# The last gate tile moves from GpSimd to VectorE, and eleven of 37 groups of heads change places

## Chip, cores and metric

The kernel runs on one core of one Trainium2 chip. The metric is the device time of one execution in microseconds (us), lower is better. The engines are called PE (TensorE), ACT (ScalarE), DVE (VectorE), POOL (GpSimd) and SP (SyncE, here only a DMA queue).

## What is computed

```python
xn = layernorm(x)                       # x: 1 x 2048 x 448, bf16
qkv = xn @ wqkv                         # 16 heads of 28
p = softmax(q @ k^T * 28**-0.5)         # 16 x 2048 x 2048
s = (p @ v) @ wo
g = silu(gelu(xn @ w1 + b1) @ w2 + b2)  # 448 -> 1792 -> 448
out = x + s * g
```

## The kernel before

**Blocks and groups.** The 16 heads are cut in four groups of four heads (g), the 2048 queries in four chunks of 512 (c). A block is one g with one c, so there are 16 blocks, run in the order b = 4g + c. A block holds 64 score tiles m of 128 keys by 512 queries: 16 key tiles times four heads. Four consecutive m, one for each head, are a group of heads q = m // 4; block b holds the groups 16b to 16b + 15. The last block is cut into narrower query pieces so that its parts finish one after the other.

**Two ways to take an exponential.** Most score tiles go from PE through PSUM to ACT: the process `p_exps` reads alternately three and two PSUM banks (512 columns each) with one ACTIVATE (line 1303). The 37 groups listed in `QUADS` (line 31) are left out of that stream (`step`) and are "late" groups: `p_late` starts one when the score stream has reached it (`K.next_m >= m0`, somewhat earlier during the GELU phase) and three work units of memory are free. DVE then computes the exponential: four TENSOR_SCALAR of 128x512 (line 1406, `p_apass`), and four instructions over 128x2048 (lines 1466, 1468, 1469, 1470, `p_expq`). A late group yields three tiles instead of one for the second matmul, so its product with v costs PE three times as many matmuls (`pv_task`, line 1542). A block's sum in the PSUM tile `acc` is complete only when all of its late groups have been added; then DVE copies it out (line 1595, `p_epi`; line 1569, `p_epi4`, for the three parts of the last block), and the next block may use `acc`.

**Order.** The order in which each engine gets its instructions is not written by hand. A planner at build time keeps a model of each engine's time, a duration and a rank for each task, and always puts next the task that can start first (`run`, `start_of`, `put`). Each engine then executes its list in that order and waits on semaphores. A change to one task, or to `QUADS`, can so reorder everything that is planned behind it. The process `p_busy` gives PE small dummy matmuls (line 919, three at a time, added to `acc` with zeros) where the model shows PE too idle; they stop when the scores are nearly at their end.

**The phases.** After loading and normalisation, blocks 0 to 8 run beside the first dense matmul (line 1111). In block 9, ACT leaves the exponentials for the GELU (line 1160). Blocks 9 to 12 run beside the second dense matmul (line 1181), whose rows end in the gate g: tanh on ACT (line 1197), then one DVE instruction. The last blocks run beside the output matmul (line 1634).

**The tail.** For the last chunk of rows (c = 3) the gate of the tiles t = 0, 1, 2 is made early. The tile t = 3 waits until the last exponential has been planned, because tanh would stand in ACT's way: tanh on ACT (line 1213), product on POOL (1215), sum on POOL (1217). In `p_epi4` and `p_norm4` the last part of the last block goes: copy out of `acc` (DVE, 1569), broadcast of the sums (PE, 1580), RECIPROCAL (DVE, 1583), product (DVE, 1586). Then `p_last` and `t_oev`: the last output matmul (PE, 1634), product with the gate (DVE, 1643), plus x (DVE, 1647), and the store (SP, 1649). The product at 1643 for t = 3 needs the gate tile t = 3 (`K.b_g3`).

`K.E_done` counts the blocks whose copy out of `acc` has been planned; it reaches `NBLK + 1` with the copy of the last part. `K.on4[3]` becomes true when the product at 1586 for t = 3 has been planned.

Of the kernel before, what the change touches and what calls it, by code (L numbers as in the profile page):

```python
# [8 lines left out]
ALU = mybir.AluOpType  # L9
ET = mybir.EngineType  # L10

PE, ACT, DVE, POOL, SP = ET.PE, ET.Activation, ET.DVE, ET.Pool, ET.SP
# [14 lines left out]
NBLK = G * C  # L27
MTOT = NBLK * T * 4

GM = 64 * 9 + 6  # L30
QUADS = (17, 21, 24, 33, 39, 49, 52, 66, 75, 85, 86, 98, 100, 114, 124, 134, 138, 142, 146, 153, 154, 155, 161, 162, 171, 178, 179, 189, 194, 197, 206, 210, 211, 225, 227, 237, 243)
SM_SCALE = DH ** -0.5
LOG2E = 1.4426950408889634
EXP_C, EXP_LC = 0.1669921875, 1.1155446
# [44 lines left out]
class _Kernel:  # L79
# [314 lines left out]
    def schedule(self):  # L394
# [28 lines left out]
        K.pv_done = [False] * MTOT  # L423
        K.late = {4 * q + k for q in QUADS for k in range(4)}
        K.late_left = [sum(1 for q in QUADS if K.sub_of(4 * q) == b) for b in range(NBLK + 3)]
        K.late_on = False
# [765 lines left out]
    def p_silu(self, c):  # L1192
        K = self
        yield ("until", lambda: K.f2n[c] == 4 and K.ready([K.b_fsb[c % 2]], 0.3) and (c < 2 or K.g_done[c - 2]))
        fb, sg = K.fsb[:, c % 2, :, :], K.sig[:, c % 2, :, :]
        nt = 4 if c < C - 1 else 3
        yield _Task(ACT, lambda eng: eng.activation(sg[:, 0:nt, :], fb[:, 0:nt, :], ACTF.Tanh, scale=0.5),
                    [K.b_fsb[c % 2]], [K.b_sig[c % 2]], 0.1 + 0.375 * nt, 0.0, 0)
        for t0 in range(0, nt, 2):
            t1 = min(t0 + 2, nt)  # L1200
            yield _Task(DVE, lambda eng, t0=t0, t1=t1: eng.scalar_tensor_tensor(
                K.g_sb[:, c, t0:t1, :], sg[:, t0:t1, :], 1.0, fb[:, t0:t1, :], op0=ALU.add, op1=ALU.mult),
                        [K.b_sig[c % 2], K.b_fsb[c % 2]], [K.b_h[c], K.b_g[c]], 0.15 + 0.467 * (t1 - t0), 0.0, 3)
        K.g_done[c] = True
        if c < C - 1:
            return
        K.b_x2[c].r = list(K.b_h[c].r) + [K.b_h[c].w]
        K.dma(SP, lambda eng: eng.dma_start(K.x2[:, c, :, :], K.A_x[0].rearrange("(c p t) d -> c p t d", p=128, t=4)[c]),
              K.s_x2[c], writes=[K.b_x2[c]])
        if nt < 4:  # L1210
            yield ("until", lambda: K.exp_m == MTOT - 1)
            o = K.g_sb[:, c, 3, :]
            yield _Task(ACT, lambda eng: eng.activation(sg[:, 3, :], fb[:, 3, :], ACTF.Tanh, scale=0.5),
                        [K.b_fsb[c % 2]], [K.b_sig3], 0.47, 0.0, 0)
            yield _Task(POOL, lambda eng: eng.tensor_tensor(o, sg[:, 3, :], fb[:, 3, :], ALU.mult),
                        [K.b_sig3, K.b_fsb[c % 2]], [K.b_h[c], K.b_g3], 0.85, 0.05, 0)
            yield _Task(POOL, lambda eng: eng.tensor_tensor(o, o, fb[:, 3, :], ALU.add),
                        [K.b_fsb[c % 2]], [K.b_h[c], K.b_g3], 0.85, 0.05, 0)

    def pieces(self, m):  # L1220
        b, r = m // 64, m % 64
# [154 lines left out]
    def p_late(self):  # L1376
        K = self
        yield ("until", lambda: K.late_on)
        K.spawn(K.p_room(), 0)
        for q in QUADS:  # L1380
            m0 = 4 * q
# [346 lines left out]
```

## Time and profile before

| what | us |
|---|---|
| median of 7 runs | 458.36 (458.24 to 459.08) |
| the profiled execution, its time | 458.41 |
| its span from first to last instruction | 456.5 |
| granted PE clock, mean | 0.997 of full |
| PE busy | 431.2 (94%) |
| ACT busy | 441.0 (97%) |
| DVE busy | 369.8 (81%) |
| POOL busy | 69.9 (15%) |

The table is read so: the span lies in the profiled execution's own time, with 1.9 us around it. Busy times are sums over the whole span, and say only which engines are nearly full. Where an engine idles, and for whom, is in the timeline (start, duration, engine, line, what is written from what, count, and in brackets the idle time before it with what ended it), in the waits (who waited for whom), and in the busy times of stretches of the span.

### The profile page before, as it was taken

The page shows a single profiled execution, that of the slowest core. Times are in us where ns is not written, and L with a number is a line of the kernel's source. Part 1 is how long each engine was busy: PE and PEld are TensorE (multiplying, and loading weights), DVE is VectorE, ACT ScalarE, POOL GpSimd, SP SyncE. Part 2 cuts the span into 40 slices and gives each one's busy share as a digit, 9 for nine tenths or more (in the row PEclk, how much of TensorE's full clock was granted, in tenths as well). Part 3 has the DMA queues.
Part 4 walks back from the last instruction along what each step waited for, and adds up shares of the span by engine and source line. Part 5 has one row for each costly group of instructions (what it writes and reads, how often), then busy time and mean ns, then how long its engine had stood idle before and what let it go on. Part 6 is the DMA issues. An engine that isn't in the chain of part 4 may idle for free.

```text
span 456.5 us, 10602 instructions
## 1 busy us (share of the span) xinstructions
PE 431.2 (94%) x4397; PEld 159.9 (35%) x4428; DVE 369.8 (81%) x574; ACT 441.0 (97%) x403; POOL 69.9 (15%) x123
## 2 busy tenths in 40 slices
PE   6999999999999999999999999999999999999995
PEld 4543323333233332323234333343333333334552
DVE  8956898958978787967879887378899889988866
ACT  6999999999999999999999998999999999999993
POOL 7470100110020101000010112020011010212211
PEclk9999999999999999999999999999999999999998
DMA  8701000000000000000040000000000000313012
GB/s 272 258 3 37 1 0 1 1 12 2 3 1 0 1 1 3 2 1 1 1 142 3 1 1 1 1 2 0 1 1 2 1 1 0 64 20 41 4 23 62
DMA packets 8049, 11.16 MB, mean 24 GB/s; under 512 B 1697, under 2 KB 6993, under 8 KB 7954
## 3 DMA queue, kind: packets, MB, share of 16 engines
q1 hardware_dynamic: 6850, 8.43, 5.8%
q0 software_dynamic: 864, 1.38, 2.5%
q8 instruction: 35, 0.57, 0.6%
q10 hardware_dynamic: 288, 0.69, 0.4%
q14 instruction: 12, 0.10, 0.1%
HBM read 8.61 MB, written 3.21 MB: 26 GB/s over the span
## 4 chain that ended last, share of the span: by engine, by line
PE 61%; ACT 24%; issue 9%; DVE 4%; DMA 1%; SPq 0%; POOL 0%; ACTq 0%; DVEq 0%; POOLq 0%
PE ring L1247 18%; ACT P L1303 13%; PE acc L1542 12%; ACT h L1303 8%; PE misc L1181 7%; PE ring L1111 6%; PE acc L919 4%; PE ring L1181 3%; PE ring L758 2%; PE misc L1111 2%; PE misc L758 1%; ACT xnT L1303 1%; PE misc L1634 1%; PE ring L1634 1%; DMA h<-in_A_wqkv_dram 1%
## 5 line engine op out<-in xcount | busy, mean ns | idle before, releaser
L1303 ACT ACTIVATE P<-ring 128x1024 bf16<-128x1024 f32 (+1 forms) x187 | 216.5, 1276 | 1.2 <-PE ring L1247 1.0
L1247 PE MATMUL ring<-qT,kT 32*128 32x512 bf16 (+2 forms) x1078 | 145.1, 358 | 10.0 <-ACT P L1303 4.5
L1303 ACT ACTIVATE h<-ring 128x1024 bf16<-128x1024 f32 (+1 forms) x102 | 118.5, 1270 | 0.4 <-PE ring L1247 0.2
L1247 PEld LDWEIGHTS ring<-qT,kT 32*128 32x128 bf16 x1078 | 37.3, 91 | 131.7 <-ACT P L1303 55.9
L1303 ACT ACTIVATE xnT<-ring 128x1536 bf16<-128x1536 f32 (+1 forms) x68 | 78.9, 1294 | 0.4 <-PE ring L1247 0.4
L1542 PE MATMUL acc<-P,vaug 128*32 128x512 bf16 (+2 forms) x530 | 49.1, 355 | 0.0
L1111 PE MATMUL ring<-xnT,w 128*128 128x512 bf16 x164 | 44.5, 381 | 2.7 <-issue 1.4
L1478 POOL TENSOR_SCALAR cv<-vaug 128x128 bf16<-128x128 bf16 x38 | 24.6, 647 | 138.3 <-PE acc L1542 136.4
L1607 POOL CAST rhi<-rc 128x16 bf16<-128x16 f32 x15 | 8.1, 537 | 200.8 <-DVE rc L1605 144.5
L1181 PE MATMUL misc<-w,h 128*128 128x448 bf16 x154 | 37.6, 356 | 0.0
L919 PE MATMUL acc<-ident,zero 128*128 128x128 bf16 x366 | 31.0, 220 | 0.0
L1542 PE MATMUL acc<-h,vaug 128*32 128x512 bf16 x248 | 28.3, 384 | 0.0
L1247 PE MATMUL misc<-qT,kT 32*128 32x512 bf16 (+1 forms) x74 | 27.7, 377 | 0.0
L919 PEld LDWEIGHTS acc<-ident,zero 128*128 128x128 bf16 x366 | 21.1, 98 | 14.6 <-issue 12.9
L1406 DVE TENSOR_SCALAR kT<-ring 128x512 uint16<-128x512 f32 x27 | 18.6, 688 | 4.6 <-PE ring L1247 4.5
L1111 PEld LDWEIGHTS ring<-xnT,w 128*128 128x128 bf16 x180 | 13.4, 97 | 21.9 <-issue 8.0
L1406 DVE TENSOR_SCALAR x_sb<-misc 128x512 uint16<-128x512 f32 x22 | 15.1, 687 | 5.6 <-PE misc L1247 5.5
L1406 DVE TENSOR_SCALAR w<-misc 128x512 uint16<-128x512 f32 x18 | 12.4, 688 | 8.4 <-PE misc L1247 8.3
L1094 DVE CAST h<-ring 128x512 bf16<-128x512 f32 x23 | 15.7, 684 | 2.8 <-PE ring L1111 2.6
L1542 PEld LDWEIGHTS acc<-P,vaug 128*32 128x32 bf16 x530 | 12.1, 95 | 15.9 <-issue 13.2
L1181 PEld LDWEIGHTS misc<-w,h 128*128 128x128 bf16 x154 | 11.2, 97 | 18.4 <-issue 11.1
L1542 PE MATMUL acc<-xnT,vaug 128*32 128x512 bf16 (+2 forms) x222 | 17.1, 332 | 0.2 <-DVE E_sb L1595 0.2
(288 smaller groups left out, 678.7 us busy)
## 6 DMA issues: line engine op xcount, KB each, us to landing
w<-in_B_w_dram SPq DMA_DIRECT2D x1, 1568.0 KB, 7.4
w<-in_B_w_dram SPq DMA_DIRECT2D x1, 1344.0 KB, 8.4
out_dram<-in_A_x_dram SPq DMA_DIRECT2D x3, 448.0 KB, 10.8
out_dram<-h POOLq DMA_DIRECT2D x6, 224.0 KB, 3.9
x_sb<-in_A_x_dram SPq DMA_DIRECT2D x2, 448.0 KB, 4.7
h<-in_A_wqkv_dram SPq DMA_DIRECT2D x3, 168.0 KB, 5.1
x_sb<-in_A_x_dram ACTq DMA_DIRECT2D x1, 448.0 KB, 5.3
h<-in_A_x_dram SPq DMA_DIRECT2D x1, 448.0 KB, 3.3
```

The source lines that it names most:

```text
L758: ins = eng.matmul(bank, w[:, kt, g * 128:(g + 1) * 128], K.xnT[:, kt, c * 512:(c + 1) * 512], start=(kt == 0), stop=(kt == KT - 1))
L919: ins = eng.matmul(K.acc[:, 0:128], K.zero[:, :], K.ident[:, :], start=False, stop=True, skip_group_check=True)
L1094: yield _Task(DVE, lambda eng: eng.tensor_copy(dst, bank), [tok], wr, 0.69, 0.0, 2)
L1111: ins = eng.matmul(bank, K.w1[:, kt, ft * 128:(ft + 1) * 128], K.xnT[:, kt, c * 512:(c + 1) * 512], start=(kt == 0), stop=(kt == KT - 1))
L1181: ins = eng.matmul(ps, hv[:, ft, t * 128:(t + 1) * 128], K.w2[:, ft, :], start=(ft == 0), stop=(ft == FT - 1))
L1247: return eng.matmul(dst, K.kT[32 * j:32 * j + 32, g, t * 128:(t + 1) * 128], K.qT[32 * j:32 * j + 32, g, c * 512 + q0:c * 512 + q0 + nq], ...
L1303: return eng.activation(reg[:, i0:i0 + n, :], K.ring[:, b0:b0 + n, :], ACTF.Exp, scale=SM_SCALE)
L1406: yield _Task(DVE, lambda eng: eng.tensor_scalar(K.unit[u][:, 512 * k:512 * k + 512].bitcast(dt.uint16), bank, SM_SCALE * LOG2E * 128.0, ( ...
L1478: yield _Task(POOL, lambda eng, i=i, t=t: eng.tensor_scalar(K.cv[:, i, :], K.vaug[:, t, 4 * g:4 * g + 4, :].rearrange("p h e -> p (h e)"), ...
L1542: return eng.matmul(K.acc[32 * j:32 * j + 32, q0:q0 + nq], w, ap[:, col:col + nq], tile_position=(0, 32 * j), start=(t == 0), stop=(t == T ...
L1607: yield _Task(POOL, lambda eng: eng.tensor_copy(K.rhi[:, :], K.rc[:, :]), [K.b_rc], [K.b_rhl], 1.1, 0.0, 1)
L1634: ins = eng.matmul(ps, K.qT[:, g, c * 512 + t * 128:c * 512 + (t + 1) * 128], K.wo[:, g, :], start=(g == 0), stop=(g == G - 1))
```

## The change

The diff does two things. The two instructions that build the last gate tile go from POOL to DVE. Each gets a place of its own: the product is offered to the planner once the last copy out of `acc` has been planned, the sum once the product at 1586 for t = 3 has been planned. Their rank becomes 2. The tanh on ACT stays.

The list of late groups changes in twelve places of 37; eleven groups leave it and eleven enter (100 is in both). Each block keeps as many late groups as it had. In blocks 1, 5 and 6 groups move later (21 to 22; 85, 86 to 87, 88; 98, 100 to 100, 101), in block 8 one earlier (134 to 133), in block 9 155 becomes 157. In block 12 the groups 197, 206 become 201, 205, in block 13 211 becomes 216, in block 14 227, 237 become 231, 238.

```diff
-QUADS = (17, 21, 24, 33, 39, 49, 52, 66, 75, 85, 86, 98, 100, 114, 124, 134, 138, 142, 146, 153, 154, 155, 161, 162, 171, 178, 179, 189, 194, 197, 206, 210, 211, 225, 227, 237, 243)
+QUADS = (17, 22, 24, 33, 39, 49, 52, 66, 75, 87, 88, 100, 101, 114, 124, 133, 138, 142, 146, 153, 154, 157, 161, 162, 171, 178, 179, 189, 194, 201, 205, 210, 216, 225, 231, 238, 243)
...
             yield _Task(ACT, lambda eng: eng.activation(sg[:, 3, :], fb[:, 3, :], ACTF.Tanh, scale=0.5),
                         [K.b_fsb[c % 2]], [K.b_sig3], 0.47, 0.0, 0)
-            yield _Task(POOL, lambda eng: eng.tensor_tensor(o, sg[:, 3, :], fb[:, 3, :], ALU.mult),
-                        [K.b_sig3, K.b_fsb[c % 2]], [K.b_h[c], K.b_g3], 0.85, 0.05, 0)
-            yield _Task(POOL, lambda eng: eng.tensor_tensor(o, o, fb[:, 3, :], ALU.add),
-                        [K.b_fsb[c % 2]], [K.b_h[c], K.b_g3], 0.85, 0.05, 0)
+            yield ("until", lambda: K.E_done == NBLK + 1)
+            yield _Task(DVE, lambda eng: eng.tensor_tensor(o, sg[:, 3, :], fb[:, 3, :], ALU.mult),
+                        [K.b_sig3, K.b_fsb[c % 2]], [K.b_h[c], K.b_g3], 0.39, 0.0, 2)
+            yield ("until", lambda: K.on4[3])
+            yield _Task(DVE, lambda eng: eng.tensor_tensor(o, o, fb[:, 3, :], ALU.add),
+                        [K.b_fsb[c % 2]], [K.b_h[c], K.b_g3], 0.39, 0.0, 2)
```

## The prediction

> **What bounds the kernel now.** I read the page's busy times first, then the busy times by stretch, then who waited for whom on ACT, then the timeline of the tail and of two stalls.
>
> ```profile
> PE 431.2 (94%) x4397; PEld 159.9 (35%) x4428; DVE 369.8 (81%) x574; ACT 441.0 (97%) x403; POOL 69.9 (15%) x123
> ```
>
> ```profile
> 300.00:340.00 40.00, 39.32 (x354) 13.67 (x354) 34.25 (x48) 39.86 (x36) 5.80 (x9) 1.00 0.01 1
> 340.00:380.00 40.00, 39.56 (x388) 12.77 (x386) 35.31 (x48) 39.57 (x35) 4.25 (x7) 1.00 0.01 1
> 380.00:420.00 40.00, 37.66 (x440) 14.43 (x437) 37.02 (x53) 40.00 (x36) 7.12 (x11) 1.00 0.19 30
> ```
>
> The columns are the stretch, its length, and busy PE, weight loads, DVE, ACT, POOL, then the granted clock. ACT is the bound: it works from 12.6 us to 449.2 us almost without a pause. The change keeps 37 late groups, and as many in each block, so ACT keeps its 876 exponential tiles and its work; what the list can win is only ACT's idle time, what it can lose is open. In 340 to 380 ACT idles 0.43 us and PE is 99% busy: there the exponentials wait for scores that stand behind other matmuls.
>
> How much is there? The trace's starts and durations give the distance between the ends of consecutive ACT instructions: 1.34 us for three banks, 0.915 for two when nothing waits. The excess over this is 4.7 us over the whole run. 1.73 us of it fall on exponentials behind the first late group of the second third (152 us on), in eight places of over 0.08 us: 0.30 at 211.6, 0.22 at 223.2, 0.12 at 277.4, 0.24 at 333.7, 0.12 at 349.7, 0.35 at 362.9, 0.09 at 365.3, 0.29 at 376.9. Beside them GELU waits 2.0 us in two places (line 1160, for PE's line 1111), at its end near 272 and 275 us.
>
> **Part 1, the tail.** The timeline of the end:
>
> ```profile
> 449.04 0.39 DVE L1647 TENSOR_TENSOR h<-h 128x448 bf16<-128x448 bf16 x1
> 449.35 0.62 DVE L1643 TENSOR_TENSOR h<-misc,h 128x448 bf16<-128x448 f32 x1
> ...
> 449.73 1.03 POOL L1215 TENSOR_TENSOR h<-w 128x448 bf16<-128x448 bf16 x1 [5.18 <-ACT w L1213]
> ...
> 450.00 1.00 DVE L1647 TENSOR_TENSOR h<-h 128x448 bf16<-128x448 bf16 x1
> ...
> 450.16 0.34 PE L919 MATMUL acc<-ident,zero 128*128 128x128 bf16 x3
> 450.84 1.06 POOL L1217 TENSOR_TENSOR h<-h,w 128x448 bf16<-128x448 bf16 x1
> 450.93 0.28 DVE L1569 CAST E_sb<-acc 128x128 bf16<-128x128 f32 x1
> ...
> 451.53 0.96 DVE L1583 RECIPROCAL w<-ring 128x128 f32<-128x128 f32 x1 [0.32 <-PE ring L1580]
> 452.59 0.29 DVE L1586 TENSOR_TENSOR qT<-E_sb,w 128x128 bf16<-128x128 bf16 x1
> ...
> 453.34 0.62 DVE L1643 TENSOR_TENSOR h<-ring,h 128x448 bf16<-128x448 f32 x1 [0.46 <-PE ring L1634]
> ```
>
> The reader is to see one instruction at two prices: line 1647 takes 0.39 us at 449.04 and 1.00 at 450.00, where POOL's product runs beside it. The copy of the last block's sum (1569) stands behind it, and the rest of the chain (1580, 1583, 1586, 1634, 1643, 1647, store) behind that copy.
>
> Removed: two POOL instructions, 1.03 + 1.06 us. They need no cover, since POOL has nothing after them. What the first does to DVE goes: 1.00 - 0.39 = 0.61 us. But the copy also waits for `acc`, whose last writers are the dummies at 450.16, ending at 450.50; an earlier copy (440.55) started 0.06 behind the last matmul (440.10 + 0.39). So PE is late next: copy at 450.56 in place of 450.93, **0.37 us earlier**. The copy itself took 0.28 here and 0.23 at 444.17; I count nothing for that.
>
> The Trainium skill (GPSIMD Engine Reference, Specifications) says that POOL shares its SBUF interfaces with VectorE and contends with DVE instructions that have two SBUF inputs. The trace agrees, 0.39 against 1.00, and 1643, whose one input is PSUM, keeps 0.62 beside the same POOL instruction. By this rule alone one would count 0.61; the wait for PE makes it 0.37. Were the dummies planned elsewhere, up to 0.6.
>
> Added: two DVE products or sums of 128x448 bf16, nearest row 1647 alone, 0.39 each. The first stands between the copy and the reciprocal. In the new times the copy ends at 450.84, the reciprocal's input comes 0.32 later, at 451.16. Unrelated DVE instructions start some 0.07 before the one ahead ends (449.04 + 0.39 = 449.43, next start 449.35), so the product runs 450.77 to 451.16 and holds the reciprocal not at all. The skill speaks against this (VectorE: DVE Perf Modes, The DRAIN you can't avoid): the next operation does not start until the pipeline is empty. By that the product would end at 450.84 + 0.39 = 451.23 and cost 0.07; this trace's overlapping starts make it 0. I take the row. The second follows 1586 (452.59 + 0.29 = 452.88, less the 0.37) and its gap to 1643 is 0.46: 0.39 fits, cost 0. If the planner put the product behind the reciprocal instead, 1586 would be 0.32 later and the gain nearly gone. ACT's tanh ends at 449.64, ahead of either place. No DMA moves; the store at 1649 only comes earlier. The part is worth -0.37, bounds -0.6 and 0.
>
> **Part 2, the list.** An exact cost cannot be read off, because the planner reorders everything behind 21. It is bounded below by the idle time (1.73 plus at most 2.0 in the GELU) and from above only by new stalls. The early moves (21, 85, 86, 98, 100) lie where ACT hardly waits: I cost them at nothing, covered by ACT's queue of finished scores; without that cover, one stall like those listed, 0.1 to 0.35. The move 155 to 157 falls in the GELU phase, where groups up to 48 tiles ahead are admitted, so 157 (tile 628, 40 beyond 588) starts as 155 did: nothing. What remains is block 12:
>
> ```profile
> 376.90 2.36 ACT L1303 ACTIVATE xnT<-ring 128x1536 bf16<-128x1536 f32 x2 [0.18 <-PE ring L1247]
> ```
>
> ```profile
> 375.01 0.40 PE L1542 MATMUL acc<-kT,vaug 128*32 128x512 bf16 x4
> 375.24 0.39 PE L1542 MATMUL acc<-wk,vaug 128*32 128x512 bf16 x4
> 375.46 0.39 PE L1542 MATMUL acc<-x_sb,cv 128*32 128x512 bf16 x4
> 375.78 0.55 PE L1181 MATMUL misc<-w,h 128*128 128x448 bf16 x2
> 376.26 0.90 PE L1247 MATMUL ring<-qT,kT 32*128 32x512 bf16 x6
> ```
>
> Before the stall at 376.9 PE works off a late group's three products (12 matmuls) and a piece of the second dense matmul. Then come the scores: of the six in the last line, three start together at 376.26 and 376.27, a fourth starts at 376.49 and ends at 376.86, two more belong to the next exponential. The fourth is the last tile of late group 206, planned into the same task; its strip of the array was taken, so it runs 0.22 behind, and ACT, which waits for the whole task, starts at 376.90. At 362.29 it is the same with a tile of 197 (fourth matmul at 362.52, ACT at 362.93); the stall at 365.3 comes with 197's last tile. Both groups leave the list. So 0.35 + 0.09 + 0.29 = **0.73 us** are at places whose cause moves away; 201 and 205 may make stalls of their own. I take the 0.73 as won and no new stall, for behind 380 us, where PE has dummies to drop, ACT shows no excess with the six groups from 210 on.
>
> **Sum.** 458.41 - 0.37 - 0.73 = 457.31, so 457.3. The profiled execution stands 0.05 above the median, which changes nothing.
>
> **Rivals.** (B) The stalls only change places: in 340 to 380 PE stays 99% busy, and 201 and 205 again have last tiles that find their strip taken. Then the tail alone counts: 458.41 - 0.37 = 458.0, no measurable difference. For it speaks that stalls appear at groups that stay, too (349.7, 333.7).
>
> (C) Slower: block 14 finishes late. Its last late group goes from 237 to 238, behind 231, which starts later than 227 did. Before, 237 was scored on DVE from 417.6 and its last step stood at 425.8, 8.2 us; the block's copy came at 429.36, while PE filled 420 to 430 with 60 dummies for want of other work. A group is 4 x 0.448 = 1.8 us of ACT; 238 then starts near 420.5 and ends near 428.7, 2.9 us later, and the copy near 432.3. All products of the last block wait for this copy. PE behind it has only some 27 dummies at 0.063 us to drop, 1.7 us, and is otherwise full to 450. Past a delay of 1.7 us the rest shows at the end: 2.9 - 1.7 = 1.2, less 0.37: 458.41 + 0.83 = 459.2; with 231 still on DVE when 238 starts, one to two us more. Against it: with 227 moved, 231 and 238 no longer share DVE with a neighbour as 225 and 227 did, and 238 may take less than 8.2.
>
> (D) PE finishes the GELU's direct tiles earlier or later, as the plan falls: up to 2.0 less or about 1 more.
>
> **Chances.** Forecast 0.42, B 0.25, C 0.28, D 0.05, half to each side. I count 0.2% (0.9 us) as what a measurement of this kernel can tell from no change: faster is below 457.4, slower above 459.3. Part of the forecast's case misses 457.4 by a small new stall, part of B passes it by a small luck. Faster 0.45, same 0.27, slower 0.28. The forecast alone ranges from 456.6 to 457.9. Down, the range takes in both bounds of part 1 and the other stalls, 458.4 - 0.6 - 1.3; up, case C with one us more, 460.2, less the tenth left out: 456.5 to 459.9.
>
> **What will show it.** Line 1647 for t = 2 at 0.39 and the copy 1569 about 0.06 behind PE's last write of `acc`; the product ahead of 1583 with the gap there unchanged; from the last exponential's end (449.2) to the span's end 6.9 in place of 7.3. For part 2: ACT's idle time in 340 to 380 at 0.1 or less in place of 0.43, and the last exponential ending near 448.5. Wrong would be a last exponential at or after 449.2, new stalls in blocks 5 to 8, or block 14's copy behind 431 with a longer tail.

## The result, and the profile after

The changed kernel takes 457.10 us (median of 12 executions, 457.01 to 457.67) against 458.42 before (30 executions): ratio 0.9970, 95% interval 0.9963 to 0.9978, 1.3 us faster. The forecast was 457.3. The sum is right; hardly one of its terms is. The executions of the first experiment below fall in two groups, four at 457.86 to 457.97 (granted clock 0.997 or 0.998) and nine at 458.26 to 458.65 (0.996), and those of before beside it likewise, 22 at 458.24 to 458.56 (0.997 to 0.999) and nine at 458.64 to 459.06 (0.995 to 0.997), so that its median compares unlike with unlike: group against group the difference is 0.4 to 0.5.

The profiled execution took 457.43 us, its span 455.6. From line 1217 on, line numbers are two higher than before. The busy times, and the stretch in which ACT idled 0.43 us before:

```profile
PE 429.5 (94%) x4389; PEld 160.6 (35%) x4419; DVE 369.1 (81%) x576; ACT 441.2 (97%) x403; POOL 69.7 (15%) x121
```

```profile
340.00:380.00 40.00, 39.45 (x387) 13.09 (x379) 35.93 (x48) 39.79 (x35) 5.05 (x7) 1.00 0.01 1
```

ACT's work is what it was, and it idles 0.21 us there in place of 0.43. The tail, from the timeline (start, duration, engine, line):

```profile
447.57 0.62 DVE L1645 TENSOR_TENSOR h<-ring,h 128x448 bf16<-128x448 f32 x1
448.22 0.39 DVE L1649 TENSOR_TENSOR h<-h 128x448 bf16<-128x448 bf16 x1
449.30 0.29 DVE L1571 CAST E_sb<-acc 128x128 bf16<-128x128 f32 x1 [0.69 <-PE acc L1544]
449.51 0.38 DVE L1216 TENSOR_TENSOR h<-w 128x448 bf16<-128x448 bf16 x1
449.92 0.96 DVE L1585 RECIPROCAL w<-misc 128x128 f32<-128x128 f32 x1
450.98 0.29 DVE L1588 TENSOR_TENSOR qT<-E_sb,w 128x128 bf16<-128x128 bf16 x1
451.19 0.38 DVE L1219 TENSOR_TENSOR h<-h,w 128x448 bf16<-128x448 bf16 x1
451.49 0.62 DVE L1645 TENSOR_TENSOR h<-ring,h 128x448 bf16<-128x448 f32 x1
452.14 0.39 DVE L1649 TENSOR_TENSOR h<-h 128x448 bf16<-128x448 bf16 x1
452.45 0.62 DVE L1645 TENSOR_TENSOR h<-ring,h 128x448 bf16<-128x448 f32 x1
453.10 0.39 DVE L1649 TENSOR_TENSOR h<-h 128x448 bf16<-128x448 bf16 x1
```

The product (1216) and the sum (1219) stand where they were expected, and cost the reciprocal nothing. But two pairs 1645, 1649 now stand behind them, where before there was one. The first belongs to tile t = 2, whose last output matmul PE now makes at 449.18, behind the last products with v; in the kernel before that pair stood ahead of the copy. Each pair takes 0.96 us from start to start. So the copy stands 1.06 us behind the last exponential's end in place of 1.74, 0.68 earlier, but from the copy to the last product it is 3.15 us in place of 2.41, 0.74 more, since t = 2's pair now stands there.

So that the parts can be told apart, I cut every trace at five points into four parts: the start of the first exponential, the start of the first GELU ACTIVATE, the end of the last one, the end of the last exponential, and the end of the last DVE instruction (2.13 or 2.14 us before the span's end in all but one run). The load of the GELU's table, 1.28 us on ACT ahead of the first ACTIVATE, counts to the first part; the expectations below that speak of 28.9 and 27.75 us count it to the GELU. Starts and ends are the trace's.

| kernel | median us | to GELU | GELU | to last exponential | tail |
|---|---|---|---|---|---|
| before | 458.42 | 235.89 | 27.58 | 173.09 | 5.21 |
| changed | 457.10 | 236.06 | 26.45 | 172.79 | 5.25 |

The differences are +0.17, -1.13, -0.30 and +0.04, together -1.22; the first exponential of this execution starts 0.30 later (12.93 against 12.63), which is why its span is only 0.9 shorter. The gain lies in the GELU stretch, for which the prediction counted nothing; the tail, for which it counted 0.37, won nothing.

### The profile page after: what moved, and what is told of

It reads as the page before. It is cut to its first block, busy times and chain, and to the rows that moved or that the text cites. A ratio compares the mean times of both kernels' runs of the same rounds, so it can differ in the third digit from the quotient of the medians.

```text
span 455.6 us, 10592 instructions
## 1 busy us (share of the span) xinstructions
PE 429.5 (94%) x4389; PEld 160.6 (35%) x4419; DVE 369.1 (81%) x576; ACT 441.2 (97%) x403; POOL 69.7 (15%) x121
## 4 chain that ended last, share of the span: by engine, by line
PE 61%; ACT 26%; issue 10%; DVE 2%; POOL 1%; ACTq 0%; DVEq 0%; POOLq 0%
PE ring L1249 17%; ACT P L1305 14%; PE acc L1544 11%; ACT h L1305 8%; PE ring L1111 7%; PE misc L1181 5%; PE ring L1181 3%; PE misc L1111 3%; ACT xnT L1305 3%; PE acc L919 2%; PE misc L758 2%; PE ring L758 2%; PE ring L1636 2%; PE misc L1636 1%; PE acc L901 1%
## 5 line engine op out<-in xcount | busy, mean ns | idle before, releaser
L1480 POOL TENSOR_SCALAR cv<-vaug 128x128 bf16<-128x128 bf16 x38 | 26.5, 698 | 134.3 <-PE acc L1544 132.6
L1111 PE MATMUL ring<-xnT,w 128*128 128x512 bf16 x139 | 35.8, 380 | 2.1 <-issue 1.4
L1181 PE MATMUL ring<-w,h 128*128 128x448 bf16 x112 | 26.9, 355 | 0.0
L1181 PE MATMUL misc<-w,h 128*128 128x448 bf16 x112 | 26.9, 355 | 0.0
L1249 PE MATMUL misc<-qT,kT 32*128 32x512 bf16 (+1 forms) x68 | 25.3, 377 | 0.0
L1111 PE MATMUL misc<-xnT,w 128*128 128x512 bf16 x68 | 19.1, 382 | 0.3 <-issue 0.2
L1111 PEld LDWEIGHTS ring<-xnT,w 128*128 128x128 bf16 x152 | 12.2, 97 | 17.7 <-issue 5.6
L1408 DVE TENSOR_SCALAR w<-ring 128x512 uint16<-128x512 f32 x17 | 11.7, 685 | 5.9 <-PE ring L1249 5.9
L1160 ACT ACTIVATE h<-h 128x2048 bf16<-128x2048 bf16 (+2 forms) x8 | 16.2, 2021 | 0.0
L1408 DVE TENSOR_SCALAR x_sb<-ring 128x512 uint16<-128x512 f32 x19 | 13.1, 687 | 3.8 <-PE ring L1249 3.8
```

What stands on the lines that cost most here:

```text
L1111: ins = eng.matmul(bank, K.w1[:, kt, ft * 128:(ft + 1) * 128], K.xnT[:, kt, c * 512:(c + 1) * 512], start=(kt == 0), stop=(kt == KT - 1))
L1160: yield _Task(ACT, lambda eng, dst=dst, src=src: eng.activation(dst, src, ACTF.Gelu_apprx_tanh), rd, wr, 0.4267 * n + (0.1 if pc else 0.06 ...
L1181: ins = eng.matmul(ps, hv[:, ft, t * 128:(t + 1) * 128], K.w2[:, ft, :], start=(ft == 0), stop=(ft == FT - 1))
L1249: return eng.matmul(dst, K.kT[32 * j:32 * j + 32, g, t * 128:(t + 1) * 128], K.qT[32 * j:32 * j + 32, g, c * 512 + q0:c * 512 + q0 + nq], ...
L1408: yield _Task(DVE, lambda eng: eng.tensor_scalar(K.unit[u][:, 512 * k:512 * k + 512].bitcast(dt.uint16), bank, SM_SCALE * LOG2E * 128.0, ( ...
L1480: yield _Task(POOL, lambda eng, i=i, t=t: eng.tensor_scalar(K.cv[:, i, :], K.vaug[:, t, 4 * g:4 * g + 4, :].rearrange("p h e -> p (h e)"), ...
```

## The experiments

The medians of before beside the runs were 458.37 (e1 to e4, e12), 458.41 (e5 to e8) and 458.34 (e9 to e11).

**The tail alone.** The changed kernel with the old list:

```diff
-QUADS = (17, 22, 24, 33, 39, 49, 52, 66, 75, 87, 88, 100, 101, 114, 124, 133, 138, 142, 146, 153, 154, 157, 161, 162, 171, 178, 179, 189, 194, 201, 205, 210, 216, 225, 231, 238, 243)
+QUADS = (17, 21, 24, 33, 39, 49, 52, 66, 75, 85, 86, 98, 100, 114, 124, 134, 138, 142, 146, 153, 154, 155, 161, 162, 171, 178, 179, 189, 194, 197, 206, 210, 211, 225, 227, 237, 243)
```

> The new tail with the old list; the instruction orders of all engines up to the last exponential are those of before. Theory P (the prediction's terms): the copy out of acc comes 0.37 us earlier, about 0.06 behind the dummies, the product is hidden ahead of the reciprocal, the sum in the gap ahead of the last product: 458.42 - 0.37 = 458.05. Theory N (the tail brings nothing, since in the changed kernel the end follows the last exponential by 7.36 us as by 7.34 before): 458.4, and an end 7.3 us behind the last exponential. Should the product hold the reciprocal up (pipeline emptied first), 458.1.

Measured: 458.31 us, ratio 0.9996 (0.9988 to 1.0004); the tail takes 4.83 us in place of 5.21. Its timeline:

```profile
449.92 0.39 DVE L1649 TENSOR_TENSOR h<-h 128x448 bf16<-128x448 bf16 x1
450.46 0.29 DVE L1571 CAST E_sb<-acc 128x128 bf16<-128x128 f32 x1
450.66 0.38 DVE L1216 TENSOR_TENSOR h<-w 128x448 bf16<-128x448 bf16 x1
451.07 0.96 DVE L1585 RECIPROCAL w<-ring 128x128 f32<-128x128 f32 x1
```

Line 1649 (1647 before) is back at 0.39; the copy starts 0.04 behind the dummies' end (450.42). From the copy's start to the reciprocal's it is 0.61, before 0.60, so the product is hidden. Step by step this is the prediction's first part. The median shows only 0.06 of it, for the reason given with the result.

**The list alone.** The change without its second half (both gate instructions stay on POOL), so the diff is the `QUADS` line of the change.

> The new list with the old tail (both gate instructions on POOL); the order up to the tail is that of the changed kernel. Theory P: the tail's 0.37 is lost again: 457.10 + 0.37 = 457.5. Theory Q (the new list puts the last output matmul of tile t = 2 behind the last products with v, so that its product and sum on DVE end up behind the last chain, and in the changed kernel both come last; in this order the product of t = 2 stands between the copy and the reciprocal): the reciprocal 0.2 later, but one product and one sum fewer behind it: 0.5 less than the changed kernel, 456.6.

Measured: 456.71, ratio 0.9962 (0.9948 to 0.9975), 0.1 above Q's number and 0.8 below P's. The parts are 236.05, 26.45, 172.80 and 4.74: as in the changed kernel but for the tail. Its order on DVE is Q's:

```profile
449.03 0.29 DVE L1569 CAST E_sb<-acc 128x128 bf16<-128x128 f32 x1 [0.69 <-PE acc L1542]
449.31 0.62 DVE L1643 TENSOR_TENSOR h<-ring,h 128x448 bf16<-128x448 f32 x1
449.85 0.95 DVE L1583 RECIPROCAL w<-misc 128x128 f32<-128x128 f32 x1
451.11 0.38 DVE L1647 TENSOR_TENSOR h<-h 128x448 bf16<-128x448 bf16 x1
451.65 0.62 DVE L1643 TENSOR_TENSOR h<-ring,h 128x448 bf16<-128x448 f32 x1 [0.16 <-PE ring L1634]
```

The product of t = 2 stands between copy and reciprocal, which comes 0.2 later for it, and behind the chain stands t = 3's pair alone. In the changed kernel the gate's product takes that place. So in this plan the new tail costs 0.39 by the medians and 0.51 by the traces; in the old it saves 0.38 by the traces.

**The front and the back of the list.** Old tail both times; first the list new up to 157, then new from 161 on:

```diff
+QUADS = (17, 22, 24, 33, 39, 49, 52, 66, 75, 87, 88, 100, 101, 114, 124, 133, 138, 142, 146, 153, 154, 157, 161, 162, 171, 178, 179, 189, 194, 197, 206, 210, 211, 225, 227, 237, 243)
```

> Old tail; the list is new up to 157 and old from 161 on. Theory P (the front of the list is worth nothing, block 12 is worth 0.73): 458.4, GELU's stretch 28.9 us long as before, and the stalls at groups 202 to 213 still there. Theory R (the trace of the changed kernel: its GELU stretch is 1.12 us shorter and the part ahead of it 0.17 longer): 458.42 - 0.95 = 457.5, GELU stretch 27.75.

```diff
+QUADS = (17, 21, 24, 33, 39, 49, 52, 66, 75, 85, 86, 98, 100, 114, 124, 134, 138, 142, 146, 153, 154, 155, 161, 162, 171, 178, 179, 189, 194, 201, 205, 210, 216, 225, 231, 238, 243)
```

> Old tail; the list is old up to 155 and new from 161 on. Theory P: the stalls of block 12 are gone, -0.73: 457.7. Theory R (behind the GELU the changed kernel's exponentials end only 0.30 us earlier, since one new stall of 0.31 stands in block 12) with the tail's order as in the list alone (0.46 shorter than before by Q): 458.42 - 0.30 - 0.46 = 457.7 too; the two differ in the trace: P has the last exponential 0.73 earlier and a tail of 7.3 us, R 0.30 earlier and a tail of 6.9. Without Q's gain 458.1.

Measured: front 457.48, ratio 0.9976 (0.9967 to 0.9985), parts 236.05, 26.46, 173.10, 5.20. Back 457.59, ratio 0.9982 (0.9974 to 0.9990), parts 235.89, 27.58, 172.78, 4.74. R holds both times. The front shortens the GELU stretch by 1.12, and lengthens the part ahead by 0.16; among ACT's new stalls there are 0.17 at 57.2 and 0.21 at 195.8 (in the changed kernel 57.4 and 196.1). The back shortens the exponentials by 0.31 and the tail, in its new order with POOL, by 0.47. In its trace the stalls at 362.9, 365.3 and 376.9 are gone, as was said, 0.73; but one of 0.31 stands at 367.7 and one of 0.11 at 439.0: -0.73 + 0.31 + 0.11 = -0.31. The same two are in the changed kernel. The timeline of the changed kernel shows why; first PE, then ACT:

```profile
366.18 0.39 PE L1249 MATMUL ring<-qT,kT 32*128 32x512 bf16 x3
366.40 0.37 PE L1249 MATMUL misc<-qT,kT 32*128 32x512 bf16 x1
```

```profile
366.82 2.37 ACT L1305 ACTIVATE P<-ring 128x1536 bf16<-128x1536 f32 x2 [0.20 <-PE misc L1249]
```

Three score matmuls start together, a fourth, into `misc`, the last tile of the new group 201, 0.22 later; ACT starts when the fourth is done (366.77). It is the stall that the prediction showed at 206 and 197, at another group.

**What the GELU stretch waits for.** Its end before, then after, PE's matmuls from the timeline:

```profile
272.23 1.03 PE L1111 MATMUL ring<-xnT,w 128*128 128x512 bf16 x4
273.18 0.40 PE L1542 MATMUL acc<-wk,vaug 128*32 128x512 bf16 x4
273.41 0.39 PE L1542 MATMUL acc<-x_sb,vaug 128*32 128x512 bf16 x4
273.62 0.39 PE L1542 MATMUL acc<-plx,cv 128*32 128x512 bf16 x4
273.95 1.04 PE L1111 MATMUL ring<-xnT,w 128*128 128x512 bf16 x4
```

```profile
272.65 1.67 PE L1111 MATMUL ring<-xnT,w 128*128 128x512 bf16 x7
274.26 0.40 PE L1544 MATMUL acc<-kT,vaug 128*32 128x512 bf16 x4
```

Before, the twelve products of a late group (273.18 to 273.95) stand ahead of the last four matmuls for which the GELU waits; after, such products stand behind them. They are not the same group's. Counted by DVE's last steps (line 1470), the ones before are 146's, whose last step ends at 272.8; after, 146's products start at 269.52, and those behind the last matmuls are 153's. The late groups have come one ahead, since the last one of block 8 is through PE sooner. The first of its three lines, before (group 134) and after (133):

```profile
251.08 0.40 PE L1542 MATMUL acc<-kT,vaug 128*32 128x512 bf16 x4
```

```profile
244.55 0.40 PE L1544 MATMUL acc<-kT,vaug 128*32 128x512 bf16 x4
```

The GELU stretch starts at 248.52 before and at 249.00 after, so 134's products lie in it and 133's ahead of it. Up to the last matmul of line 1111, PE makes 60 products in the stretch before and 48 after. On ACT these are the only waits of the GELU that the timeline shows, before and after:

```profile
272.51 1.45 ACT L1160 ACTIVATE h<-ring 128x1536 bf16<-128x1536 f32 x1 [0.88 <-PE ring L1111]
275.08 1.02 ACT L1160 ACTIVATE h<-ring 128x1024 bf16<-128x1024 f32 x1 [1.12 <-PE ring L1111]
```

```profile
272.72 1.45 ACT L1160 ACTIVATE h<-ring 128x1536 bf16<-128x1536 f32 x1 [0.52 <-PE ring L1111]
274.43 1.02 ACT L1160 ACTIVATE h<-ring 128x1024 bf16<-128x1024 f32 x1 [0.25 <-PE ring L1111]
```

Two experiments test what the twelve are worth. The first holds the products of late groups back that PE makes early, while direct tiles (the GELU's input that ACT reads straight from PSUM, line 1111) are still to come, in the kernel before:

```diff
-            low = lambda: q % 16 > 0 and K.E_done >= first - 1 and len(K.free_u) < 3 and any(K.ready(K.b_U[x[1][2]]) for x in mine())
+            low = lambda: not (K.in_gelu() and K.dir_n >= ND - 3) and q % 16 > 0 and K.E_done >= first - 1 and len(K.free_u) < 3 and any(K.ready(K.b_U[x[1][2]]) for x in mine())
```

> The kernel before, list and tail unchanged; only the early products of late groups (p_pv's condition low) are held back while the last direct tiles of the GELU are still to come, so that PE makes the last four matmuls of line 1111 ahead of group 153's twelve products and not behind them. Theory R (the front of the list won by this order at the GELU's end): the GELU's stretch 0.8 to 1.0 shorter than 28.9 us, time 457.5. Theory S (it won by a smaller backlog of late groups in blocks 5 to 8, which leaves less for the GELU): stretch and time as before, 458.4.

(The twelve products called 153's there are 146's, as counted above.) Measured: 463.93, ratio 1.0118 (1.0104 to 1.0131). The GELU stretch is 26.71, 0.87 shorter, as R has it, with nothing changed ahead of it (235.90): the twelve now start at 274.20, behind the last direct tile, and the last wait is 0.25 in place of 1.12, the one before it 0.88 as it was. But the part behind takes 179.42, 6.3 us more: the planner laid everything behind the GELU anew, and in the new plan ACT waits where it did not before. The two worst places, ACT's timeline, and DVE's beside the first:

```profile
388.72 2.36 ACT L1303 ACTIVATE P<-ring 128x1536 bf16<-128x1536 f32 x2 [2.35 <-PE acc L1542]
392.42 1.45 ACT L1303 ACTIVATE P<-ring 128x1536 bf16<-128x1536 f32 x1 [1.34 <-PE acc L1542]
```

```profile
388.67 0.68 DVE L1470 TENSOR_SCALAR x_sb<-x_sb 128x2048 uint16<-128x2048 uint16 x1
390.08 0.69 DVE L1595 CAST E_sb<-acc 128x512 bf16<-128x512 f32 x1 [0.72 <-PE acc L1542]
```

Late group 206, the fifteenth of 16 in block 12, is ready at 388.67 + 0.68 (in the kernel before its last step started at 381.9); `acc` cannot be copied until 390.08; ACT has no free place to write to, and waits for products with v. This is the mechanism of rival C, in another block.

The second moves one group only:

```diff
-QUADS = (17, 21, 24, 33, 39, 49, 52, 66, 75, 85, 86, 98, 100, 114, 124, 134, 138, 142, 146, 153, 154, 155, 161, 162, 171, 178, 179, 189, 194, 197, 206, 210, 211, 225, 227, 237, 243)
+QUADS = (17, 21, 24, 33, 39, 49, 52, 66, 75, 85, 86, 98, 100, 114, 124, 133, 138, 142, 146, 153, 154, 155, 161, 162, 171, 178, 179, 189, 194, 197, 206, 210, 211, 225, 227, 237, 243)
```

> The kernel before with one group moved, 134 to 133; the planned order then has the last sixteen matmuls of line 1111 in a row. Theory R: GELU's stretch about 1 us shorter, 457.4, nearly all that the front of the list won. Theory S (all the moves of blocks 5, 6 and 8 are needed): at most a third of it, 458.1.

Measured: 458.79, ratio 1.0005 (0.9996 to 1.0013): neither. 133's products stand ahead of the GELU as in the changed kernel (from 241.17), the last sixteen matmuls of line 1111 do follow each other, and the last wait is again 0.25; but the GELU stretch is 27.80, longer than before. ACT waits 0.62 ahead of the last wait, and in two new places:

```profile
260.81 1.45 ACT L1160 ACTIVATE h<-ring 128x1536 bf16<-128x1536 f32 x1 [0.41 <-PE ring L1111]
267.57 1.45 ACT L1160 ACTIVATE h<-ring 128x1536 bf16<-128x1536 f32 x1 [0.80 <-PE misc L1602]
```

PE is busy in all of the stretch:

```profile
248.66:276.46 27.80, 27.80 (x198) 10.07 (x195) 25.65 (x36) 25.72 (x17) 4.32 (x6) 1.00 0.00 1
```

In this stretch scores keep PE busy for 4.80 us (14 matmuls) against 3.47 (12) before. So the stretch is as long as the work that PE has ahead of its last direct tile. Twelve products fewer there take 0.87 off the last wait: in e5_hold by their order at the end, theory R; in the changed kernel because one late group less is left for the GELU, which is theory S's cause, and e5_hold could not tell the two apart. The remaining 0.26 of the 1.13 lies at the wait before it, 0.52 in place of 0.88, less some 0.1 lost elsewhere; why PE is there sooner was not taken apart. The move from 134 to 133 alone takes the group out of the stretch, but in its plan two more score matmuls come in; which of the front's other moves keep them out stays open.

**The place of t = 2.** In the changed kernel, the first part of t = 3's output matmul is held back until t = 2's is complete:

```diff
-        bank, tok = yield ("bank", lambda: K.g_done[c] and (K.on4[t] or (pre and K.exp_m >= MTOT - 7)))
+        bank, tok = yield ("bank", lambda: K.g_done[c] and (K.on4[t] or (pre and K.wo2)))
...
-        yield K.t_wo(ps, tok, c, t, (3,), 3)
+        yield K.t_wo(ps, tok, c, t, (3,), 0.5 if t == 2 else 3)
+        if t == 2:
+            K.wo2 = True
```

> The changed kernel; the first part of the last output matmul of tile t = 3 is held back until that of t = 2 is complete, so that t = 2 is through PE ahead of the last products with v and its product on DVE ahead of the last copy out of acc. Theory Q (in the changed kernel t = 2's product and sum, 0.96 us from start to start, stand behind the last chain and give the tail's gain back): the last product on DVE 0.6 earlier, time 456.5. Theory N (the end is set by the chain copy, reciprocal, product, matmul, whatever stands beside it): 457.1.

Measured: 456.72, ratio 0.9957 (0.9944 to 0.9969), 0.38 less than the changed kernel. Q holds at two thirds of its size: the product of t = 2 stands at 448.52, ahead of the copy, but its sum still stands behind the chain, and the copy comes 0.18 later (449.48), since the matmul moved ahead now delays the products with v. The tail is 4.79 against 5.25. This version and the list alone are faster than the changed kernel by the same 0.4.

> The changed kernel with both edits of the two runs before. In its plan 18 matmuls of line 1111 follow each other at the GELU's end, ahead of all late products. If the two effects are separate and R and Q hold: e7_wo_first's time less 0.4 to 0.8 of the 1.2 us that the GELU still waits for PE: 455.7 to 456.1. If the products held back only come due behind the GELU and are paid there: as e7_wo_first.

Measured, with both edits: 459.13, ratio 1.0014 (1.0006 to 1.0023). The GELU stretch is 25.81, another 0.64 shorter, and the part behind 175.71, 2.92 longer, in eleven stalls of 0.1 to 0.6 from 312 us on. As in e5_hold, a gain in mid-schedule is more than paid back behind it, in a plan that the list was not chosen for.

**Front and new tail together.** The changed kernel with e3_list_front's list:

> The new tail on e3_list_front's list (new up to 157, old from 161 on). The planned order of the tail is that of e1_tail_only, so if the tail's 0.38, read from that run's trace, is real and adds: 457.48 - 0.38 = 457.10, the changed kernel's time without the changes in blocks 12 to 14, and a last product on DVE that ends 4.83 us behind the last exponential. If the median of e1_tail_only (0.06 less than before) is right and the trace is not: 457.4.

Measured: 457.13, ratio 0.9971 (0.9960 to 0.9983), tail 4.83. The tail's gain is real, 0.35 by the medians of this run and e3_list_front, 0.37 by their traces. And the changed kernel's time is reached without the changes in blocks 12 to 14: these win 0.30 at the exponentials and lose 0.42 in the tail.

**POOL beside DVE.** In the kernel before, the gate's product on POOL gets the condition of the change:

```diff
+            yield ("until", lambda: K.E_done == NBLK + 1)
             yield _Task(POOL, lambda eng: eng.tensor_tensor(o, sg[:, 3, :], fb[:, 3, :], ALU.mult),
```

> The kernel before; the two gate instructions stay on POOL, but the first waits, as in the change, until the last copy out of acc has been planned. Theory P (the tail's 0.37 comes from line 1647 no longer running beside POOL): the copy again 0.06 behind the dummies, so the last product on DVE would be 0.37 earlier, but POOL's 1.03 + 1.06 us start near 450.8 and end near 452.9, when the last product comes due: 0.3 to 0.37 less than before, 458.1, as with the engine changed. Theory M (the move to DVE itself is what counts): the product at 1586, with two SBUF inputs, and the last product now wait for POOL, 458.4 or more.

Measured: 458.32, ratio 0.9999 (0.9991 to 1.0007), and the trace is that of before: POOL starts at 449.74, line 1648 takes 1.00. Neither theory was tested. The condition holds the planner, not POOL: no semaphore follows from it. On DVE the same condition works because DVE's list then has the product behind the copy. With a real wait:

```diff
-                        [K.b_sig3, K.b_fsb[c % 2]], [K.b_h[c], K.b_g3], 0.85, 0.05, 0)
+                        [K.b_sig3, K.b_fsb[c % 2], K.b_E4[3]], [K.b_h[c], K.b_g3], 0.85, 0.05, 0)
```

> e9_pool_gated with a real dependency: POOL's gate product also reads the last copy of acc, so that POOL waits on DVE's semaphore and cannot start beside line 1647. Theory P (the 0.37 is line 1647's stretch beside POOL): 1647 takes 0.39, the copy stands 0.06 behind the dummies, 0.37 earlier than before. POOL then works from about 450.9 to 453.0: its sum meets the product at 1586, which has two SBUF inputs and would be stretched, and the last product comes due at 453.0. Net between 0.37 less than before (1586 keeps 0.29) and 0.2 more (1586 stretched by the 0.6 that 1647 was): 458.0 to 458.5. Theory O (1647's stretch has another cause, such as its wait for x): 1647 stays at 1.00 and the time at 458.3.

Measured: 458.77, ratio 1.0009 (1.0003 to 1.0016), tail 5.58. DVE's timeline, then POOL's:

```profile
450.06 0.39 DVE L1648 TENSOR_TENSOR h<-h 128x448 bf16<-128x448 bf16 x1
450.59 0.29 DVE L1570 CAST E_sb<-acc 128x128 bf16<-128x128 f32 x1
451.21 0.96 DVE L1584 RECIPROCAL w<-ring 128x128 f32<-128x128 f32 x1 [0.32 <-PE ring L1581]
452.27 1.04 DVE L1587 TENSOR_TENSOR qT<-E_sb,w 128x128 bf16<-128x128 bf16 x1
```

```profile
451.04 1.02 POOL L1216 TENSOR_TENSOR h<-w 128x448 bf16<-128x448 bf16 x1 [6.44 <-DVE E_sb L1570]
452.14 1.03 POOL L1218 TENSOR_TENSOR h<-h,w 128x448 bf16<-128x448 bf16 x1
```

With POOL out of its way 1648 is back at 0.39 and the copy 0.39 earlier against the last exponential's end; then the product at 1587, beside POOL's second instruction, takes 1.04 in place of 0.29, so that the tail is 0.37 longer (-0.39 + 0.75). The longer time goes where POOL goes. That is Theory P's mechanism, and Theory O is out; but P's range ended at 458.5, 0.2 more than before, and the median is 0.40 more: 1587 was stretched by 0.75, not by 0.6.

**Only free strips.** In the kernel before, a late score tile may join the stream's task only where a strip of the array is free:

```diff
-        if len(rows) == 4 or len(p["rs"]) > 1:
+        if len(rows) == 4 or len(p["rs"]) > 1 or all(K.pieces(m)[1] in rows for m in r["left"]):
```

> The kernel before; a score tile of a late group may join the task of the score stream only where a strip of the array is free, otherwise it is planned as a task of its own. Theory F (the single stalls of the exponentials, 0.2 to 0.35 us, are fourth matmuls that run behind the first three on a taken strip): no excess of over 0.2 us at three-bank exponentials between 100 us and the GELU; time between 457.2 and 458.4, as the plan falls behind. Rival (the stalls come from PE being full, whatever rides along): as many such places as before (two between 200 and 240 us, four between 330 and 380), time 458.4 or more.

Measured: 471.83, ratio 1.0292 (1.0278 to 1.0306), above both theories' times. From 125 us to the GELU ACT shows no wait for PE and no three-bank excess of over 0.2, as F has it; but one of 0.32 stands at 100.5, and new waits outweigh all, as the list of ACT's waits shows (waited for, us in total, times, longest):

```profile
ACT P L1303 <- PE acc L1542: 3.5, 2, 2.4
ACT h L1303 <- PE ring L1247: 2.9, 2, 2.7
```

The plan was laid anew from the first late groups on, so its time does not decide F. Its matmuls' starts settle one half of it. In the kernel before, four score matmuls of 512 columns start together 59 times, and 17 times three start together and the fourth 0.22 or 0.23 later; in this run it is 74 times and none. So the delay is that of a taken strip. The other half, that ACT waits for this fourth matmul, is read at the stalls of 362.9 and 376.9 before and of 366.8 after; what all such stalls cost together stays open.

All runs in the parts of the first table:

| run | median us | to GELU | GELU | to last exponential | tail |
|---|---|---|---|---|---|
| e1_tail_only | 458.31 | 235.90 | 27.58 | 173.09 | 4.83 |
| e2_list_only | 456.71 | 236.05 | 26.45 | 172.80 | 4.74 |
| e3_list_front | 457.48 | 236.05 | 26.46 | 173.10 | 5.20 |
| e4_list_back | 457.59 | 235.89 | 27.58 | 172.78 | 4.74 |
| e5_hold | 463.93 | 235.90 | 26.71 | 179.42 | 5.20 |
| e6_133 | 458.79 | 236.12 | 27.80 | 173.09 | 5.21 |
| e7_wo_first | 456.72 | 236.05 | 26.46 | 172.79 | 4.79 |
| e8_wo_hold | 459.13 | 236.05 | 25.81 | 175.71 | 4.83 |
| e9_pool_gated | 458.32 | 235.90 | 27.58 | 173.09 | 5.20 |
| e10_front_tail | 457.13 | 236.05 | 26.46 | 173.10 | 4.83 |
| e11_free_strip | 471.83 | 238.78 | 27.97 | 181.32 | 6.17 |
| e12_pool_waits | 458.77 | 235.89 | 27.58 | 173.09 | 5.58 |

## Why the prediction was right, and where it was not

**Part 1** was right in mechanism and size for the plan that it was worked out on: 0.37 forecast, 0.38 in e1_tail_only, with PE's dummies next and the product hidden for nothing. By the Trainium skill's sentence that was set against it (VectorE: DVE Perf Modes, The DRAIN you can't avoid) the product would have cost 0.07; it cost 0.01 at most. The same section lets a next operation that is not held start earlier, and the trace agrees: the product starts at 450.66, 0.09 before the copy ends. The step that failed is the unsaid one, that the tail's order stays. The list, treated as a matter of the exponentials alone, changed the tail's order (4.74 with the old gate instructions), and with the new ones t = 2's pair came to stand behind the chain: the term is +0.04 in place of -0.37. From the last exponential's end to the span's end it is 7.4 us, not the 6.9 announced.

**Part 2, block 12.** "I take the 0.73 as won and no new stall": the 0.73 went, and 0.42 of new stalls came, one of the very kind that the prediction had just explained, at one of the two groups that it named as doubtful. The term measures -0.30 to -0.31. ACT's idle time in 340 to 380 is 0.21, where 0.1 or less was to show it.

**Part 2, the front.** "I cost them at nothing" failed, by the largest amount: -0.96 (+0.17 ahead of the GELU, -1.13 in it). The reason given, that ACT hardly waits where the groups stand, looked for the effect at the place of the move. It lies in the GELU, where PE is busy for 27.18 of 27.60 us: one late group fewer that PE has to work off there takes 0.87 off ACT's last wait. The group is that of block 8, and its move from 134 to 133 the prediction does not cost at all. The GELU's 2.0 us of waiting had been read and named as rival D, at 0.05. The front was run only as a whole and as 134 to 133: whether 157 is worth nothing, as forecast, is neither shown nor refuted. A sign named for being wrong did come, a new stall of 0.22 in block 7 (196.1), beside others there that shrank.

**The sum** came out by luck, because three errors cancel: the terms were off by +0.41, +0.43 and -0.96, together -0.12. The traces differ by 1.22 and the medians by 1.32, where 1.10 was forecast. Rival C did not happen in block 14 (its copy came at 426.3, three microseconds earlier than before, not later). That it can happen is shown by e5_hold.

## What to carry to other kernels

Where a planner orders everything, price an edit in each stage behind it and not only where it stands: cut the traces of both kernels at the same few events, and test each part of the change alone before believing that they add. The same tail edit was worth -0.35 with one list and +0.39 with another. And a condition in the planner is not a wait on the chip: it changes the order of one queue, and holds another engine back only if a semaphore follows from it.

## What the runs showed of the hardware

A DVE instruction with two SBUF inputs that started behind one of POOL's was held until that was over. The one of 0.39 us ended at 451.00, 0.24 behind POOL's (450.76); the one of 0.29 at 453.31, 0.14 behind (453.17): each its own length, less 0.15, behind POOL's end. Instructions with one PSUM input kept their times (0.62 for 1643, 0.96 for the reciprocal). The Trainium skill (GPSIMD Engine Reference, Specifications) says that the two contend; that the price is about the rest of POOL's instruction is what these two runs show.

It goes the other way, too. In the kernel before, DVE's product of 128x2048, both of its inputs in SBUF, and POOL's subtraction beside it and alone:

```profile
130.98 1.23 DVE L1468 TENSOR_TENSOR kT<-w 128x2048 f16<-128x2048 bf16 x1
```

```profile
131.08 1.20 POOL L1608 TENSOR_TENSOR rlo<-rc,rhi 128x16 bf16<-128x16 f32 x1
154.59 0.22 POOL L1608 TENSOR_TENSOR rlo<-rc,rhi 128x16 bf16<-128x16 f32 x1
```

Here DVE was first, and POOL's small instruction ended 0.07 behind it. In all three places where 1608 starts beside such a product it takes 1.20, and 0.22 elsewhere. So it was the later of the two that paid. How much of an instruction counts is open: at 269.71 a DVE product behind one of POOL's of 0.53 lost only 0.08.

A score matmul of 512 columns on a strip of the array that is taken starts 0.22 or 0.23 us behind the three beside it: 17 times in the kernel before, never in e11_free_strip, where no tile joins on a taken strip. ACT's exponential starts only when it is done (366.77, then ACT at 366.82).
